# K and Q of tiles 4 to 15 projected with the tokens as the stationary operand, and laid out by transposing DMAs

## The chip, the cores and the metric

The kernel runs on one core of a Trainium2 chip. The metric is the device time of one execution in microseconds (us). The core has five engines with an instruction queue each: PE (matrix multiplication), ACT (activation functions, copies out of PSUM), DVE (element-wise vector work), POOL (a slower vector engine that can't read PSUM) and SP, which here does nothing but issue DMAs. Every queue is executed in its order: an instruction that waits holds up all those behind it on its engine.

## The reference: what is computed

One layer with two branches over x of 2048 rows (S) and 448 columns (D). Both branches are modulated by vectors that come from c: `sa, ca, ga, sb, cb, gb`, the six slices of `silu(c) @ w_mod`.

```python
h = _layernorm(x) * (1 + ca) + sa
q, k, v = h @ wqkv                      # 16 heads of 28 columns
scores = q k^T * 28 ** -0.5             # key j for row i only if 0 <= i - j < 256
o = softmax(scores) v
x = x + ga * (o @ wo)
h = _layernorm(x) * (1 + cb) + sb
z = gelu(h @ w_in)                      # 1792 columns; z1 the first 896, z2 the last
g = w_sp @ layernorm(z2) + b_sp         # w_sp: 2048 x 2048, over the rows
x = x + gb * ((z1 * g) @ w_out)
```

## The kernel before

**Tiles and stages.** The rows are cut into 16 tiles of 128; four tiles make a block (`tb`, 0 to 3). The attention window of 256 keys lets a tile see itself and the two tiles before it. There is one kernel-wide program, and its stages overlap:

1. Loads, modulation vectors, layernorm of x. For tiles 4 to 15 the normalised rows (`xn`) are brought into the layout with columns on partitions (`hT`) by a transposing DMA per tile (named h1 below; `turn`, line 465), and the modulation is applied to `hT` per block (lines 730 and 732). Tiles 0 to 3 are transposed on PE.
2. Projections. Weights for Q and K lie in `WQK`, where each head of 28 columns is padded to 32 so that a head starts on a partition that is a multiple of 32. The weights are the stationary operand and the tokens stream past: the result comes out with head columns on partitions, as the scores need it. Q of tiles 4 to 15 is made per block, four groups of four matmuls of 512 tokens (line 763, evicted into `qT` at 772 or 773), and copied once more into `QBD`, a block-diagonal arrangement for one part of the scores (lines 790 and 791). K is made per tile, 16 matmuls of 128 tokens (line 821), and evicted into `KT` (833 or 834). V has the tokens stationary and the weights streaming, four matmuls of 448 columns per tile (line 841), and is evicted into `Vaug` (845 or 846).
3. Attention of tile j, in two halves of eight heads: score matmuls (line 956, and 967 for a part that takes `QBD`; 926 for tiles 0 and 1), the exponential on ACT (line 912), a mask multiplication on DVE (973 and 993), the product with V (line 1000), division by the row sum (1014 and 1016), a transposing DMA of the result into `hT` (named o below), the product with wo (line 1026, `mo`), the residual sum (1030), the second layernorm, and another transposing DMA into `hT` (named h2).
4. The mixer. Line 1120 makes z2, line 1141 makes z1. w_sp comes from DRAM by 32 transposing DMAs of 128 x 1024, 16 into `wspA` and 16 into `wspB`. The matmuls over rows (line 1166) start when all of z2 and `wspA` are there; line 1185 is the product with w_out.

**Memory.** Most of the on-chip memory is shared by things that live at different times. `wspA` overlays `qT` and `QBD` in its first half, `wspB` overlays `KT` and `PT`.

**What sets the order.** Nothing is scheduled at run time. The kernel lists its operations (`Sched.add`; 1148 of them), with the engines that could run each, and what each depends on. `PLAN` is a text that gives the finished order: `a`, `d`, `t`, `p` and `s` stand for ACT, DVE, POOL, PE and SP, the number is the operation's place in the list, and numbers behind a dot choose buffers. `order()` hands each engine its operations in that order, `waits()` puts in the semaphore waits. So a new PLAN moves work between ACT, DVE and POOL and within every queue. SP's part of the old PLAN, from the first transpose on, in words (`h1_4`: normalised rows of tile 4 into `hT`; `o_0`: attention output of tile 0; `h2_0`: second normalisation of tile 0; `wA`, `wB`: slices of w_sp; in brackets, plain loads):

```
h1_4 h1_6 h1_7 h1_5 (x3) h1_8 h1_10 (wo) o_0 wA11 h1_9 o_1 h1_11 (winh1) wA14 o_2 wA13 o_3 (winh0) h1_13
(win1) o_4 h1_15 h1_12 h1_14 o_5 o_6 (win0) h2_0 wA15 o_8 o_7 (win2) h2_2 wA10 o_9 h2_1 o_10 h2_3 h2_6 o_11
h2_4 o_12 o_13 h2_7 o_14 h2_5 (wout) wA5 wA6 o_15 h2_8 h2_9 h2_10 h2_11 wB4 wA4 wA3 h2_12 h2_14 h2_13 wA12
h2_15 wA8 wA2 wA7 wA9 wA0 wB8 wA1 wB15 wB9 wB14 (bsp) and the eleven other wB
```

Of the kernel before, what the change touches and what calls it, by code (L numbers as in the profile page):

```python
# [12 lines left out]
a0 t30 d24 s1 d27 d26 d25 d23 d22 p51.1 t31 p60.3 s2 t32 p52.2 t35 p59.0 s4 p61.1 p55.0 s6 a3 p58.0 p63.0 a5  # L13
s10 t36 p40.1 a7 s8 p69.2 a9 p75.3 d114 s12 p65.1 p53.0 t33 d112 p68.2 s11 t34 p54.3 d115 p77.0 d113 p50.3 s13
a41 p71.0 t116 a43 p46.0 s15 d117.0 t29 p74.2 d118.3 p62.0 p64.2 p47 a42 a44 p57.0 p48.1 d106 d86 p76.0 p49
a107 t104 p129.6 p67.3 d87 d105 p126.4 t37 a130 p82.3 p56.3 t111 p84.1 d127 p81.1 p73.1 a131 p83.3 p66.0 d128
t38 p72.0 p141.1 d110 d121 p78.0 a108 t109 p70.2 p150.3 d119 p142 d122 d120 p79.2 d184 p151 t123 a143 p138.0
a152 t28 d125.2 p139 d124.3 p85.0 p147.6 d178 a140 p132.2 d185 p148 d182 a133 p144.7 d179 d180 p135.1 a134
p153.0 d183 a136 d181 p371.0 d246 t186 a137 p145 d248 p154 a372.4 t39 p165.1 d187.3 t190 d242 s194 p166 t188
a149 t192 d45 p377.0 a146 d373 p156.6 d167 a378.6 t189.1 p157 d244 p159.7 t191.2 a158 p395.0 d193.0 a155 s196  # L20
d379 p172.6 a396.5 d249 d247 p173 d243 p175.1 a174 s197 p160 d88 t89 d245 a397 p176 d168 p94.0 t250 p95 d177
s195 a171 p402.0 a161 d96 t254 p97.1 t256 a403.1 p98 d398 s14 d375 p162.7 d400 p374.0 p163 a404 d381 p90.0 d99
p376 d201 a199 p422.0 d198 d251.0 p380 p382 d200 p91 s258 a423.0.0 p211.1 d93 d92 d407 d170 d252 p212 p218.0
d255.1 t253.2 a164 d383 s260 p429.0 d169 a213 t257.3 p219 a430.3 p399.1 p205.1 s16 d220 p206 d384.2 p202.0
d306 s385 p203 a207 d426 p401 p447.0 a204 p208.1 s804 a448.4.1 d310 p209 d405 p227.0 d431 p228 s259 t102
p424.1 p406 p408 a425 p454.0 d229 a210 d409 p427.0 d312 a455.1 p230.0 t101 d410.1 p221.1 p231 d216 d214 d451
# [223 lines left out]
def bass_adaLN_cond__sliding_block__mixer_gmlp__prompt_kernel(  # L250
# [84 lines left out]


    QBD, _, qbd_bytes = alloc("QBD", [128, 2, 4, 2, 256], BF16, at=wspA_off)
    qT, _, qt_bytes = alloc("qT", [128, 2, 4, 512], BF16, at=wspA_off + qbd_bytes)
    assert qbd_bytes + qt_bytes <= NT * HS * 2

    z2, z2_off, z2_bytes = alloc("z2", [128, NT, FH], BF16)
# [927 lines left out]
```

## Time and profile before

| | |
|---|---|
| three runs | 276.32, 274.94, 275.12 us; median 275.12 |
| profiled execution, first to last instruction | 273.2 us (its own time is given as this span; 1.9 us less than the median of the runs) |
| busy: PE, ACT, DVE, POOL | 98%, 46%, 59%, 41% of the span |
| transposing DMAs into `hT` | 28 from `xn` and `xn2`, 16 from `o_sb` |
| transposing DMAs of w_sp | 32 |

How to read it: the profile is one execution, its times are microseconds from the first instruction. A line such as L821 is a line of the kernel. In the windows each engine has its busy time in a stretch, with the number of its instructions in brackets. PE's busy time counts a matmul until its last result is out, so single matmuls overlap and a mean of 0.2 us for one does not mean that it holds PE for so long; how long a group holds PE is read from the chain of waits, where each piece lasts until the next one begins. In the timeline of SP a row is the issue of a DMA, with its start, its length on SP and, where rows of one kind are merged, their number; the landing is told by tile.

### The profile page before, as it was taken

The page shows a single profiled execution, that of the slowest core. Times are in us where ns is not written, and L with a number is a line of the kernel's source. Part 1 is how long each engine was busy: PE and PEld are TensorE (multiplying, and loading weights), DVE is VectorE, ACT ScalarE, POOL GpSimd, SP SyncE. Part 2 cuts the span into 40 slices and gives each one's busy share as a digit, 9 for nine tenths or more (in the row PEclk, how much of TensorE's full clock was granted, in tenths as well). Part 3 has the DMA queues.
Part 4 walks back from the last instruction along what each step waited for, and adds up shares of the span by engine and source line. Part 5 has one row for each costly group of instructions (what it writes and reads, how often), then busy time and mean ns, then how long its engine had stood idle before and what let it go on. Part 6 is the DMA issues. An engine that isn't in the chain of part 4 may idle for free.

```text
span 273.2 us, 8371 instructions
## 1 busy us (share of the span) xinstructions
PE 267.1 (98%) x3741; PEld 155.3 (57%) x3751; DVE 160.4 (59%) x344; ACT 126.4 (46%) x149; POOL 111.4 (41%) x147
## 2 busy tenths in 40 slices
PE   8999999999999999999999999999999999999996
PEld 6976676777667866554554444444444444444453
DVE  3798999989889999949889210221222022152244
ACT  5799999899989988567666400000000000000000
POOL 6455298305033286547448003354543023061330
PEclk9999999999999999999999999999999999999999
DMA  7999846453234573957789996000000000001003
GB/s 209 299 244 132 127 103 122 122 101 109 64 103 67 91 73 72 185 117 134 117 176 175 217 186 118 0 0 0 2 0 0 0 2 0 34 17 36 34 34 118
DMA packets 67301, 25.54 MB, mean 93 GB/s; under 512 B 58497, under 2 KB 66178, under 8 KB 67266
## 3 DMA queue, kind: packets, MB, share of 16 engines
q1 hardware_dynamic: 66016, 24.02, 44.5%
q10 hardware_dynamic: 1250, 0.99, 1.3%
q8 instruction: 29, 0.48, 0.7%
q14 instruction: 6, 0.05, 0.1%
HBM read 9.01 MB, written 1.84 MB: 40 GB/s over the span
## 4 chain that ended last, share of the span: by engine, by line
PE 80%; ACT 8%; DMA 6%; DVE 3%; SPq 2%; issue 1%
PE ps L1166 35%; PE ps L1120 8%; PE ps L1141 8%; PE ps L1185 8%; ACT PW L912 6%; DMA wmodB<-in_w_mod_dram 6%; PE ps L1000 5%; PE ps L956 4%; PE ps L1026 4%; PE ps L763 3%; PE ps L821 2%; PE ps L841 2%; DVE PT L973 1%; ACT QBD L790 1%; PE ps L967 1%
## 5 line engine op out<-in xcount | busy, mean ns | idle before, releaser
L1173 POOL TENSOR_TENSOR z1T<-tmpg,z1T 128x512 bf16<-128x512 bf16 x28 | 32.0, 1152 | 77.3 <-DVE tmpg L1170 77.3
L912 ACT ACTIVATE PW<-ps 128x2048 bf16<-128x2048 f32 (+1 forms) x42 | 59.9, 1452 | 5.4 <-PE ps L956 3.9
L1170 DVE TENSOR_TENSOR tmpg<-ps,bsp_bc 128x512 bf16<-128x512 f32 x28 | 18.9, 689 | 73.8 <-PE ps L1166 62.6
L1166 PE MATMUL ps<-wspB,z 128*128 128x512 bf16 x219 | 49.7, 379 | 0.3
L1166 PE MATMUL ps<-wspA,z 128*128 128x512 bf16 x219 | 49.1, 379 | 0.4 <-issue 0.2
L633 POOL TENSOR_TENSOR rs_all<-mv_all,neghalf 128x1 f32<-128x1 f32 (+2 forms) x37 | 22.5, 635 | 45.6 <-DVE mv_all L631 45.6
L1166 PEld LDWEIGHTS ps<-wspA,z 128*128 128x128 bf16 x224 | 21.8, 98 | 26.6 <-issue 0.4
L1166 PEld LDWEIGHTS ps<-wspB,z 128*128 128x128 bf16 x224 | 21.9, 98 | 26.2
L973 DVE TENSOR_TENSOR PT<-PW,mask 128x2048 bf16<-128x2048 bf16 x28 | 34.0, 1219 | 0.0
L1000 PE MATMUL ps<-Vaug,PT 128*128 128x32 bf16 x496 | 25.8, 177 | 0.0
L1000 PEld LDWEIGHTS ps<-Vaug,PT 128*128 128x128 bf16 x496 | 22.9, 96 | 3.3 <-issue 0.4
L1120 PE MATMUL ps<-w_in,hT 64*128 64x448 bf16 x224 | 22.0, 349 | 0.0
L1185 PE MATMUL ps<-w_out_g,z1T 128*128 128x448 bf16 (+2 forms) x119 | 22.0, 341 | 0.0
L1141 PE MATMUL ps<-hT,w_in 64*128 64x512 bf16 x196 | 22.0, 376 | 0.0
L1000 PE MATMUL ps<-Vaug,PW 128*128 128x32 bf16 x224 | 21.2, 176 | 0.0
L629 DVE BATCH_NORM_STATS2 st_all<-z 128x6 f32<-128x448 bf16 x32 | 18.4, 608 | 4.4 <-ACT z L1127 4.3
L629 DVE BATCH_NORM_STATS2 st_all<-x_sb 128x6 f32<-128x448 bf16 x32 | 19.2, 614 | 2.7 <-DMA x_sb<-in_A_x_dram 2.5
L1195 DVE TENSOR_TENSOR fin<-ps,x_sb 128x448 bf16<-128x448 f32 (+1 forms) x16 | 9.5, 612 | 16.7 <-PE ps L1185 11.6
L1000 PEld LDWEIGHTS ps<-Vaug,PW 128*128 128x128 bf16 x224 | 17.9, 96 | 1.9
L821 PE MATMUL ps<-hT,WQK 112*128 112x128 bf16 x256 | 18.7, 219 | 0.0
L1149 ACT ACTIVATE z1T<-ps 128x512 bf16<-128x512 f32 x28 | 14.5, 603 | 8.8 <-PE ps L1141 8.7
L956 PE MATMUL ps<-qT,KT 32*128 32x128 bf16 (+5 forms) x1344 | 17.1, 197 | 0.9 <-ACT PW L912 0.6
(108 smaller groups left out, 355.0 us busy)
## 6 DMA issues: line engine op xcount, KB each, us to landing
wmodB<-in_w_mod_dram SPq DMA_DIRECT2D x1, 1568.0 KB, 15.3
out_dram<-fin SPq DMA_DIRECT2D x14, 112.0 KB, 1.7
x_sb<-in_A_x_dram SPq DMA_DIRECT2D x3, 448.0 KB, 7.9
w_in<-in_B_w_in_dram SPq DMA_DIRECT2D x3, 448.0 KB, 4.2
w_out_g<-in_B_w_out_dram SPq DMA_DIRECT2D x1, 784.0 KB, 6.4
bsp_bc<-in_B_b_sp_dram SPq DMA_DIRECT2D x1, 512.0 KB, 5.3
x_sb<-in_A_x_dram SPq DMA_DIRECT2D x2, 224.0 KB, 4.9
hT<-xn SPq DMA_TRANSPOSE x28, 2.9
```

The source lines that it names most:

```text
L629: st = [dve(0.62, lambda e, t=t, o=12 - 6 * (n - ci), s=s: e.bn_stats(st_all[:, slot, t, o:o + 6], s()), deps(t), prio) for ci, s in enume ...
L633: return pool(0.4 + 0.15 * len(tiles), lambda e: e.tensor_tensor(rs_all[:, slot, a:b], mv_all[:, slot, a:b, 1], neghalf[:, 0:b - a], ALU.pow),
L821: km = lambda g, kc, start, stop, h=h, t=t: lambda e: e.matmul(ps[:, h.slot[0], g * 128:(g + 1) * 128], lhsT=WQK[0:CP, kc, 16 + 4 * g:20 + ...
L912: ex = act(xdur, lambda e, out_ap=out_ap, in_ap=in_ap: e.activation(out_ap(), in_ap(), ACT.Exp, scale=SCALE), [s] + list(after), v - 8.0 + ...
L956: fm.append(lambda e, hm=hm, qi=qi, key=key, kn=kn, lo=lo, hi=hi, col=col, p0=p0, t=t, j=j: e.matmul(ps[p0:p0 + kn, hm.slot[t], col:col + ...
L973: mk2 = lock_d(1.2, lambda e, hp=hp, at_w=at_w, pad=pad, at_f=at_f, cols=cols, j=j: e.tensor_tensor(cols(hp.slot[0] * 2048, [[256, 8], [12 ...
L1000: fns.append(lambda e, hp=hp, hO=hO, hi=hi, bi=bi, kb=kb, hd=hd, nb=nb, a=at[hi][bi], p_of=p_of: e.matmul(ps[:, hO.slot[0], 32 * hd:32 * h ...
L1120: return lambda e, kc, p0, start, stop: e.matmul(ps[:, hs[t % 2].slot[hf], 0:D], lhsT=hT[p0:p0 + 64, kc, t * 128:(t + 1) * 128], rhs=w_in[ ...
L1141: return lambda e, kc, p0, start, stop: e.matmul(ps[:, hs[b // 2].slot[b % 2], :], lhsT=w_in[p0:p0 + 64, kc, ft * 128:(ft + 1) * 128], rhs ...
L1166: m = pe(16 * MMS, [lambda e, h=h, si=si, ft=ft, tb=tb: e.matmul(ps[:, h.slot[0], :], lhsT=z2[:, si, ft * 128:(ft + 1) * 128], rhs=(wspA i ...
L1173: u = pool(1.16, lambda e, ht=ht, ft=ft, tb=tb: e.tensor_tensor(z1T[tb][:, ft, :], tmpg[:, ht.slot[0], :], z1T[tb][:, ft, :], ALU.mult), [ ...
L1185: return [lambda e, ft=ft: e.matmul(ps[:, h.slot[0], 0:hi - lo], lhsT=z1T[t // 4][:, ft, (t % 4) * 128:(t % 4 + 1) * 128], rhs=w_out_g[:, ...
```

## The change

- For tiles 4 to 15, K and Q are projected like V: the 128 tokens of a tile are stationary and 448 unpadded weight columns stream past, four matmuls each. The weights are taken straight from where they were loaded (`wq_st`, which gets a place of its own).
- The results have tokens on partitions. K is evicted, with its heads spread to 32 columns, into a staging tile `kst` (two of them), and a transposing DMA of 128 x 512 lays it into `KT`. Q is evicted in two parts, of 224 columns each, into a staging tile `qst` of ten blocks of 128 columns, in which the block-diagonal arrangement is already spread out among zeros; a transposing DMA of 128 x 1280 lays it into `qring`. The QBD copies of these tiles go.
- `KT` becomes a ring of eight tiles, Q a ring of four. K of tile t waits for the scores that used its place, and so does Q.
- `qT` and `QBD` are kept for tiles 0 to 3, whose projections stay as they were; they now overlay part of `w_in`, so two loads of `w_in` wait for the scores of tiles 0 to 3.
- The first eight slices of `wspA` overlay the Q ring and wait for all scores. Five `wspA` slices had been issued before attention output 14; now it is two.
- ACT zeroes one half-size `QBD` instead of two; POOL zeroes the two `qst` and the padding of the two `kst`.
- Rules that paced the old projections (`PACE`, `LEAD`) go. PLAN is new: the first loads stay in the old order, everything later was searched anew. There are 1175 operations. SP's part, from the first transpose on (`k_4`, `q_4`: K and Q of tile 4):

```
h1_4 h1_5 h1_7 h1_6 (wo) h1_11 h1_10 q_6 q_4 h1_8 h1_9 k_4 o_0 o_1 k_5 q_5 (winh1) q_7 k_6 o_2 h1_12 o_3 k_7
q_8 h1_13 q_9 h1_14 k_8 h1_15 (winh0) q_10 k_9 (win1) q_11 o_5 o_6 o_4 k_11 k_10 wA14 h2_1 o_7 wA13 q_12 o_8
q_13 k_12 (win0) o_9 (win2) k_13 h2_3 q_14 h2_0 q_15 o_10 k_14 h2_4 h2_2 o_11 k_15 o_12 o_13 h2_5 h2_7 h2_6
o_14 wA4 (wout) h2_9 h2_8 wA11 o_15 h2_11 wA5 wA8 h2_10 wA12 wA10 h2_12 h2_14 h2_15 h2_13 wA7 wA9 wB4 wA0
wB8 wA6 wA15 wA1 wA2 wB15 wA3 wB9 wB14 (bsp) and the eleven other wB
```

The core of the diff (the PLAN is left out, and the removed per-block projection is cut):

```diff
-    KT, kt_off, kt_bytes = alloc("KT", [128, 4, S], BF16)
+    KR, QR, QB_N = 8, 4, 10
+    KT, kt_off, _ = alloc("KT", [128, 4, KR * 128], BF16)
+    wq_st, _, _ = alloc("wq_st", [128, DC, 2 * D], BF16)
+    kst = [alloc("kst0", [128, H, 32], BF16)[0]]
...
+    qring, _, qr_bytes = alloc("qring", [128, QR, QB_N, 128], BF16, at=wspA_off)
+    qst, _, qs_bytes = alloc("qst", [128, 2, QB_N * 128], BF16, at=wspA_off + qr_bytes)
...
+    t_qsz = [pool(0.8, lambda e, i=i: e.memset(qst[:, i, :].bitcast(F32), 0.0), prio=-60.0) for i in range(2)]
+    t_ksz = [pool(0.2, lambda e, i=i: e.memset(kst[i][:, :, DH:32], 0.0), prio=-60.0) for i in range(2)]
...
-            mms = [lambda e, h=h, g=g, kc=kc, tb=tb: e.matmul(
-                ps[:, h.slot[0], :], lhsT=WQK[0:CP, kc, 4 * g:4 * g + 4, :].rearrange("p a b -> p (a b)"),
-                rhs=hT[0:CP, kc, tb * 512:(tb + 1) * 512], start=(kc == 0), stop=(kc == DC - 1)) for kc in range(DC)]
...
+                def by_tokens(part, h, t=t, evs=evs, v=v):
+                    return pe2(4 * MMD, [lambda e, kc=kc: e.matmul(
+                        ps[:, h.slot[0], 0:D], lhsT=hT[0:CP, kc, t * 128:(t + 1) * 128], rhs=wq_st[0:CP, kc, part * D:(part + 1) * D],
+                        start=(kc == 0), stop=(kc == DC - 1)) for kc in range(DC)], [evs, (t_wk, t_wq)[1 - part]], v + 1, [h])
...
+                K_ready[t] = turn("d_k%d" % t, lambda t=t: KT[:, :, t % KR * 128:(t % KR + 1) * 128], lambda hs=hs: kst[hs.slot[0]][:].rearrange("p h e -> p (h e)"), [ev], v + 1)
...
+                    q_evs.append(either(
+                        0.37, lambda e, q_in=q_in, q_to=q_to: e.activation(q_to(), q_in(), ACT.Copy),
+                        0.35, lambda e, q_in=q_in, q_to=q_to: e.tensor_copy(q_to(), q_in()), [m, t_qsz], v + 1, [] if odd else [hs]))
...
+                Q_ready[t] = turn("d_q%d" % t, lambda t=t: qring[:, t % QR], lambda hs=hs: qst[:, hs.slot[0], :], [q_evs], v + 1, lat=1.6)
...
+    for t in range(8, NT):
+        K_ready[t].deps.update(x for i in range(t - KR, t - KR + 3) for x in S_of[i])
+        Q_ready[t].deps.update(S_of[t - QR])
+    for op in t_win_l[:2]:
+        op.deps.update(x for i in range(4) for x in S_of[i])
+        op.deps.update(q_dma)
```

More of the change, by code (lines that the diff above doesn't have):

```diff
@@ L18 @@
[L18 to L22, printed above, removed]
@@ L1020, in bass_adaLN_cond__sliding_block__mixer_gmlp__prompt_kernel @@
         hO.until += [rec, t_o]
[L1022 to L1023 removed]
+        oe = turn("d_oT%d" % j, lambda j=j: hT[:, :, j * 128:(j + 1) * 128], lambda ho=ho: o_sb[:, ho.slot[0], :], [t_o, hT_used[j]], v - 9.0)
         ho.until.append(oe)
```

298 lines of the change are left out of this document (136 added, 162 removed).

## The prediction

> **What bounds the kernel now.** I read the page first, then busy times by windows, the chain of waits, and the timeline of SP, which issues the transposing DMAs.
>
> ```profile
> span 273.2 us, 8371 instructions
> ...
> PE 267.1 (98%) x3741; PEld 155.3 (57%) x3751; DVE 160.4 (59%) x344; ACT 126.4 (46%) x149; POOL 111.4 (41%) x147
> ```
> ```profile
> 40.00:60.00 20.00, 19.48 (x576) 14.28 (x577) 18.06 (x35) 18.11 (x19) 8.64 (x9) 1.00 0.56 118
> 60.00:80.00 20.00, 19.75 (x589) 14.28 (x588) 17.88 (x32) 18.26 (x18) 4.27 (x6) 1.00 0.31 76
> 80.00:100.00 20.00, 19.36 (x629) 15.29 (x626) 19.74 (x40) 18.17 (x18) 9.45 (x16) 1.00 0.55 93
> ```
>
> The page's time is one execution of 273.2 us; the median of three runs is 275.12, so 1.9 us lie outside the span, and I add my difference to 275.12. The windows (length, then busy PE, weight load, DVE, ACT, POOL, clock, share of the DMA engines) show attention filled by PE, with DVE and ACT over 88% busy beside it and the DMA engines half used. PE's idle time is 0.52, 0.25 and 0.64 us in 20: what is taken from DVE or ACT alone can give back 1.4 us in these 60 at most. What is taken from PE counts in full, if everything that feeds PE keeps step.
>
> ```profile
> 26.58 1.04 PE ps L763 x4
> ...
> 53.23 0.90 PE ps L821 x16
> ...
> 65.25 0.76 PE ps L841 x4
> ...
> 68.75 0.87 PE ps L763 x4
> ...
> 101.94 0.61 PE ps L956 x32
> ...
> 152.73 10.74 PE ps L1166 x49
> ```
>
> In the chain of waits (start, length) a tile's K projection takes 0.90 us of PE (L821, 16 matmuls), a tile's quarter of a block's Q projection 0.87 (L763), and the V projection, which has its tokens stationary already, 0.76 (L841). At 101.94 stands the first score group of the last tile, tile 15; from it PE runs almost without a gap to 152.73, the first matmul with w_sp, 50.8 us later. Everything behind that is unchanged.
>
> **PE.** K and Q of tiles 4 to 15 become two projections of V's form. K falls from 0.90 to 0.76, Q from 0.87 to 0.76: 0.25 us in each of 12 tiles, 3.0 us, if PE stays the bound.
>
> **Evictions.**
>
> ```profile
> L846 DVE CAST Vaug<-ps 128x448 bf16<-128x448 f32 x6 | 3.6, 604 | 0.2 <-PE ps L841 0.2
> L834 DVE CAST KT<-ps 128x512 bf16<-128x512 f32 x5 | 3.4, 679 | 1.9 <-PE ps L821 1.7
> L791 DVE COPY QBD<-qT 32x512 bf16<-32x512 bf16 x7 | 3.3, 472 | 0.2
> ```
>
> Per tile before, at DVE's prices: one K of 512 columns (0.68), a quarter of four Q of 512 (0.68), a quarter of four QBD copies (0.47): 1.83 us. After: one K of 448 columns (0.60) and two Q halves of 224. The first two rows differ by 75 ns in 64 columns, so a half costs about 0.34: 1.28 in all. Twelve tiles save 6.6 us over DVE and ACT together. I count it at nothing, since PE's idle time allows 1.4 us; that end goes into the range.
>
> **Zeroing at the start.** ACT's second QBD fill goes, and POOL gets four memsets behind its first `rs_all`, ahead of the small `o_sb` memset and a copy into WQK.
>
> ```profile
> 1.66 1.21 POOL L499 MEMSET Vaug<- 128x768 bf16 x1
> ...
> 5.80 0.26 POOL L491 MEMSET o_sb<- 128x192 bf16 x1
> 8.41 0.56 POOL L617 COPY WQK<-wq_st 112x448 bf16<-112x448 bf16 x1 [2.36 <-DMA wq_st<-in_A_wqkv_dram]
> ```
>
> Two of 640 words and two of 64 columns cost between 4 x 0.26 and 2 x 1.21 + 2 x 0.26, 1.0 to 2.9 us, under 2.36 us in which POOL waited for a load. Their cover is that load; if it came earlier, or the memsets took the upper price, the first K matmuls would start up to 0.6 us later. I take nothing, the nearer row being the short one.
>
> **SP, the queue of the transposes.** All DMAs of this stretch are issued by SP, in one order. The change adds 24 transposes: 12 of K (four blocks of 128 x 128, like those into hT) and 12 of Q (ten blocks). Each waits for its evictions, and behind it in SP's order wait transposes of normalised rows, attention output and w_sp, and through them hT, `mo` and the last stage; the score groups wait for the new ones themselves.
>
> ```profile
> 16.65 7.39 SPq L465 DMA_TRANSPOSE hT<-xn  x4
> ...
> 30.57 1.19 SPq L465 DMA_TRANSPOSE hT<-o_sb  x1
> 31.80 1.83 SPq L465 DMA_TRANSPOSE wspA<-in_B_w_sp_dram  x1
> ...
> 65.32 0.58 SPq L432 DMA_DIRECT2D w_in<-in_B_w_in_dram  x1
> ...
> 87.59 1.20 SPq L465 DMA_TRANSPOSE hT<-o_sb  x1
> 88.87 1.88 SPq L465 DMA_TRANSPOSE hT<-xn  x1
> 91.20 1.19 SPq L465 DMA_TRANSPOSE hT<-o_sb  x1
> 92.44 2.88 SPq L465 DMA_TRANSPOSE hT<-xn  x2
> 95.36 1.27 SPq L465 DMA_TRANSPOSE hT<-o_sb  x1
> 97.05 2.15 SPq L465 DMA_TRANSPOSE hT<-xn  x1
> ...
> 104.77 1.55 SPq L465 DMA_TRANSPOSE hT<-xn  x1
> 106.36 1.27 SPq L465 DMA_TRANSPOSE hT<-o_sb  x1
> ...
> 116.48 5.19 SPq L465 DMA_TRANSPOSE hT<-xn  x4
> ...
> 143.20 1.29 SPq L465 DMA_TRANSPOSE wspA<-in_B_w_sp_dram  x1
> ...
> 149.38 16.93 SPq L465 DMA_TRANSPOSE wspB<-in_B_w_sp_dram  x11
> ```
> ```profile
> L465 SPq DMA_TRANSPOSE hT<-xn x28: 1188/1265/2212, 16.6 to 132.7; - x28
> ...
> DMA to landing us min/median/max: 2.3/3.0/6.6
> ```
>
> Four transposes in a row took 5.19 us at 116.48: with the gap behind, 1.31 us of SP for each, whatever else is free. A load takes 0.58, 0.62 with its gap. Between the first transpose at 16.65 and that of attention output 14 at 106.36 the old order has 38 transposes and seven loads, 54 us of 90: SP mostly waits. The new order has 60 and six there, 82 us, and PE means to be done with the stretch in 87.
>
> Does a Q transpose of ten blocks cost SP 1.31, or 2.5 times that? wspA's, of eight blocks, took 1.29 at 143.20, against 1.27 for four: I take 1.31 and keep the other end as a rival.
>
> Some issues are longer: 1.88 at 88.87, 2.15 at 97.05. Of the 33 transposes from 30.57 to 106.36 eight took over 1.5 us, the first at 31.80, the last at 104.77, and together 4.7 over their share: 0.14 for each of the 33. A queue that never pauses can't dodge these.
>
> The sum follows SP to the K transpose of tile 15, the last input of the score group at 101.94. Ahead of it, from 16.65, stand 54 transposes and six loads: 54 x 1.31 + 6 x 0.62 = 74.5. The first Q transpose, of tile 6, is the eighth in the order: by count 25.1. Its input can't be there: Q of this block starts at 26.58 on PE, and 0.76 of matmuls, the pipeline and an eviction half bring it to about 28.1. SP stands for 3.0. The longer issues add 54 x 0.14 = 7.6. So it is issued at 16.65 + 74.5 + 3.0 + 7.6 = 101.7 and lands 3.0 later by the median, 104.7: 2.8 us behind the old 101.94, while PE, 3.0 ahead, stands idle for some 5 us over tiles 12 to 15. Its queue is in order, so all work behind the score group waits too. Counted by the chain's spacings, the new order keeps 0.6 us less PE work behind this point. That gives 2.8 - 0.6 = 2.2 us over before, 277.3.
>
> At 116.48 transposes are spaced by their issue and not by their movement, and that is the ground of this sum. The Trainium skill (DMA: Bandwidth & Descriptors, Issuing engines are not separate DMA queues) says that the sequencer's time to initiate a DMA is usually small beside the DMA; here it is 1.27 of a landing of 3.0. By that rule SP would not be a bound, and the first rival would hold.
>
> For movement: eleven wspB transposes of 256 KB took 16.93 us, 1.54 each, so eight blocks move in at most that and ten in 1.9. A tile's K and Q then add 0.8 + 1.9 = 2.7 us of all DMA engines, 32 us in 85, upon shares of 0.31 to 0.56. That stays under one, but landings get later than the median; the range takes that in. The Trainium skill (Advanced Engine Details and Errata, X-Bar Transpose (TRN2)) expects 350 to 400 GB/s; the row gives 170. By its figure the addition would be half as long, and landings would hold to the median.
>
> Loads of w_in now wait for the scores of tiles 0 to 3; those are over before the first is due, and their place in SP's order is in the count.
>
> **Rivals.** *SP keeps step, PE stays the bound.* If pauses before SP's early inputs are shorter, the long issues are rarer, or the K transposes are ready with spare time, PE gets its 3.0 us: 272.1; with the 1.4 us of idle time, 270.7. For it: 82 us of SP fit into 87. Against: that leaves 5 for 3.0 of waiting and 60 x 0.14 = 8.4 of long issues. It decides at an issue of tile 15's K by about 96. Chance 0.31.
>
> *Saving and lag cancel.* The forecast with a lag of SP that is 1 to 3 us smaller, 274.3 to 276.3, no change. Chance 0.25.
>
> *The transposes of w_sp arrive last.*
>
> ```profile
> L465 SPq DMA_TRANSPOSE wspA<-in_B_w_sp_dram x16: 1166/1301/4177, 31.8 to 143.2; - x16
> ...
> DMA to landing us min/median/max: 3.0/3.9/6.7
> ```
>
> Behind attention output 14 the old order has 24 issues to the last wspA transpose, in 143.20 - 106.36 = 36.8 us; landing by 147.1, it had 5.6 us to spare before 152.73. The new one has 27 (early wspA transposes have moved behind): 41.4. With SP late, output 14 goes at 16.65 + 82.3 + 3.0 + 8.4 = 110.4, the last wspA at 151.8, landing at 155.7 to 158.5; PE would want it at 152.7 + 2.2 = 154.9. That is 0.8 to 3.6 us beyond the forecast, 278.1 to 280.9. It decides from a landing later than PE's 154.9. Chance 0.12, beside the forecast's own 0.29.
>
> *A ten-block issue costs 2.5 times a four-block one:* 12 x 1.9 = 23 us, 298. The 1.29 speaks against it; 0.03.
>
> That the change does not save PE time I exclude: V's form is in the trace.
>
> **How the numbers follow.** A difference under 0.5% (1.4 us) can't be told from none here. The edges are 273.7 and 276.5, and the forecast, 277.3, stands over the upper one: slower 0.29 + 0.12 + 0.03 = 0.44, same 0.25, faster 0.31. Slower is likelier than same, since the two terms that carry the lag, landing and long issues, can grow with a fuller queue and hardly shrink. The range runs from 271.8, short of the first rival's best end, to 280.3, inside the third's; some 0.2 is left out at both ends. The forecast's own range, over a lag of SP that is up to 2 us shorter or longer, is 275.3 to 279.3.
>
> **What would show it.** Right: SP's timeline without pauses from 45 to 105; transposes into KT landing 3 us or more after issue; among PE's waits, the score groups for DMA into KT or the Q ring, several us in all; K and Q projections at 0.76 us a tile; tile 15's first scores between 103 and 106; the first w_sp matmul at 153 to 156. Wrong: SP waiting for several us in each 20, PE at 19.5 or more in each window to 100, and the first w_sp matmul before 151. If PE waits for wspA ahead of its first w_sp matmul, it is the third rival.

## The result, and the profile after

The changed kernel is slower: 299.5 us median against 275.7 for the kernel before, beside it on the same chip. Medians are over all runs, while ratios leave out disturbed, slower runs: two of the four here (301.5 and 301.8), two of four in e16_vector_later and one each in e6_k_alone, e7_sixteen_less and e17_start_mended. The ratio is 1.073 (95% interval 1.065 to 1.081), 20 us. The profiled execution of the changed kernel took 294.6 us, and its page begins:

```profile
span 292.8 us, 8134 instructions
...
PE 271.6 (93%) x3597; PEld 149.6 (51%) x3607; DVE 159.9 (55%) x340; ACT 121.1 (41%) x144; POOL 119.4 (41%) x159
```

PE's share fell from 98% to 93%. The windows show where, in the columns of the prediction's (length, then busy PE, weight load, DVE, ACT, POOL, granted clock, share of the DMA engines):

```profile
40.00:60.00 20.00, 16.73 (x511) 10.99 (x498) 16.96 (x34) 15.38 (x16) 11.04 (x11) 1.00 0.70 114
60.00:80.00 20.00, 17.05 (x504) 11.73 (x499) 17.14 (x27) 16.35 (x14) 8.57 (x8) 1.00 0.99 151
80.00:100.00 20.00, 17.79 (x424) 10.84 (x424) 15.69 (x31) 12.23 (x12) 2.90 (x6) 0.91 0.82 133
```

From 40 to 100 us PE now stands for 3.3 + 2.9 + 2.2 = 8.4 us, where it stood for 1.4. Its waits (us in all, times, longest), the largest and those that the prediction named:

```profile
PE ps L1010 <- DVE KT L796: 4.0, 1, 4.0
PE ps L966 <- DMA KT<-kst: 3.0, 2, 1.8
...
PE ps L1165 <- DMA wspA<-in_B_w_sp_dram: 1.4, 1, 1.4
```

The first is new and stands at the start; the second is a score group that waits for the transposed K; the third is the first matmul with w_sp (L1165) waiting for a slice of w_sp. SP's timeline (start, length on SP, merged issues), at the start and at the end of the attention part:

```profile
16.61 6.65 SPq L471 DMA_TRANSPOSE hT<-xn  x4
23.30 0.58 SPq L399 DMA_DIRECT2D wo_g<-in_A_wo_dram  x1
29.55 2.50 SPq L471 DMA_TRANSPOSE hT<-xn  x2
33.80 3.96 SPq L471 DMA_TRANSPOSE qring<-qst  x2
...
109.71 1.67 SPq L471 DMA_TRANSPOSE KT<-kst  x1
111.42 2.58 SPq L471 DMA_TRANSPOSE hT<-xn  x2
114.04 1.85 SPq L471 DMA_TRANSPOSE hT<-o_sb  x1
115.93 1.28 SPq L471 DMA_TRANSPOSE KT<-kst  x1
```

The first Q transpose goes out at 33.80 and the last K transpose at 115.93. Between them an issue begins some 0.04 us after the one before has ended; all that goes beyond this is 0.4 us together. At the start SP still pauses, 5.7 us ahead of 29.55.

What the trace shows best is when each score group starts on PE. From the timelines of PE, in us (the experiments in the columns are told below):

| first matmul of | before | after | e4 | e5 | e15 | e9 | e17 | e11 |
|---|---|---|---|---|---|---|---|---|
| tile 2 | 25.1 | 34.1 | 33.1 | 24.7 | 35.6 | 26.9 | 26.0 | 26.5 |
| tile 4 | 37.1 | 45.3 | 45.2 | 36.7 | 47.5 | 45.0 | 39.9 | 45.5 |
| tile 9, second half | 69.8 | 83.3 | 78.0 | 78.2 | 88.8 | 81.7 | 79.2 | 77.8 |
| tile 15 | 101.9 | 119.3 | 110.1 | 114.6 | 125.6 | 120.5 | 116.2 | 108.7 |
| w_sp | 152.7 | 172.4 | 160.9 | 169.5 | 180.2 | 173.1 | 171.7 | 162.4 |
| span | 273.2 | 292.8 | 281.4 | 290.2 | 300.9 | 293.8 | 292.4 | 283.1 |

The changed kernel loses 8.2 us by tile 4, 9.2 more by tile 15, 2.3 more by the first matmul with w_sp, and nothing behind it. So there are two losses to explain, an early one and a long one, and my theory had only the second.

The early one can be read in the chain of waits (start, length) of the changed kernel:

```profile
8.29 14.77 DMA x_sb<-in_A_x_dram
...
23.09 0.63 DVE st_all L637
...
26.80 0.58 DVE KT L796
27.37 0.05 issue
27.42 0.29 PE ps L1010 x4
```

DVE's new order has the statistics (L637) of tiles 13 to 15 ahead of masks and of the eviction of K of tile 2 (L796). These tiles belong to the last third of x, whose load lands at 23.1, so DVE stands for 5.5 us in front of it with ready work behind, and PE behind DVE for 4.0. So my theory, A below, has two parts: an early loss by the order at the start, and a long one by SP's full queue. The main rivals: the loss is PE's own, in the new projections and evictions; the issues are long because of Q's ten blocks; or SP's pauses would take the new issues in, and the order alone is at fault. All ratios are to the kernel before, run beside it on the same chip, with a 95% interval; "us more" is worked out from them.

### The profile page after: what moved, and what is told of

It reads as the page before. It is cut to its first block, busy times and chain, and to the rows that moved or that the text cites. A ratio compares the mean times of both kernels' runs of the same rounds, so it can differ in the third digit from the quotient of the medians.

```text
span 292.8 us, 8134 instructions
## 1 busy us (share of the span) xinstructions
PE 271.6 (93%) x3597; PEld 149.6 (51%) x3607; DVE 159.9 (55%) x340; ACT 121.1 (41%) x144; POOL 119.4 (41%) x159
## 4 chain that ended last, share of the span: by engine, by line
PE 48%; DMA 18%; DVE 11%; POOL 8%; SPq 8%; issue 3%; ACT 2%; POOLq 0%; DVEq 0%
PE ps L1165 33%; PE ps L1184 7%; SPq L471 6%; DMA x_sb<-in_A_x_dram 5%; DMA hT<-o_sb 3%; DMA KT<-kst 3%; DMA hT<-xn 3%; DVE PT L983 2%; POOL xn L659 2%; DVE st_all L637 2%; POOL hT L1060 2%; PE ps L805 2%; ACT PW L922 2%; POOL rs_all L641 2%; DMA wspA<-in_B_w_sp_dram 2%
## 5 line engine op out<-in xcount | busy, mean ns | idle before, releaser
L1165 PE MATMUL ps<-wspA,z 128*128 128x512 bf16 x219 | 49.1, 379 | 1.6 <-DMA wspA<-in_B_w_sp_dram 1.4
L1165 PE MATMUL ps<-wspB,z 128*128 128x512 bf16 x219 | 49.7, 379 | 0.3
L641 POOL TENSOR_TENSOR rs_all<-mv_all,neghalf 128x1 f32<-128x1 f32 (+2 forms) x37 | 24.9, 697 | 46.8 <-DVE mv_all L639 44.5
L1165 PEld LDWEIGHTS ps<-wspA,z 128*128 128x128 bf16 x224 | 21.8, 98 | 27.8 <-issue 1.6
L1165 PEld LDWEIGHTS ps<-wspB,z 128*128 128x128 bf16 x224 | 21.9, 98 | 26.2
L983 DVE TENSOR_TENSOR PT<-PW,mask 128x2048 bf16<-128x2048 bf16 x28 | 34.8, 1255 | 0.8 <-ACT PW L922 0.8
L1010 PEld LDWEIGHTS ps<-Vaug,PT 128*128 128x128 bf16 x496 | 22.7, 96 | 9.1 <-DVE KT L796 4.4
L805 PE MATMUL ps<-wq_st,hT 112*128 112x448 bf16 x96 | 24.9, 382 | 0.6 <-DVE kst L818 0.6
L637 DVE BATCH_NORM_STATS2 st_all<-x_sb 128x6 f32<-128x448 bf16 x32 | 18.9, 613 | 8.1 <-DMA x_sb<-in_A_x_dram 8.0
L637 DVE BATCH_NORM_STATS2 st_all<-z 128x6 f32<-128x448 bf16 x32 | 18.2, 605 | 4.0 <-ACT z L1126 4.0
L966 PE MATMUL ps<-qring,KT 32*128 32x128 bf16 (+5 forms) x1152 | 15.4, 201 | 5.2 <-DMA KT<-kst 3.0
L966 PEld LDWEIGHTS ps<-qring,KT 32*32 32x32 bf16 (+1 forms) x1152 | 12.1, 92 | 13.2 <-ACT PW L922 5.4
L1035 PE MATMUL ps<-wo_g,hT 112*128 112x448 bf16 x64 | 17.1, 378 | 1.6 <-DMA hT<-o_sb 0.7
```

The costliest lines, as they stand in the source:

```text
L637: st = [dve(0.62, lambda e, t=t, o=12 - 6 * (n - ci), s=s: e.bn_stats(st_all[:, slot, t, o:o + 6], s()), deps(t), prio) for ci, s in enume ...
L641: return pool(0.4 + 0.15 * len(tiles), lambda e: e.tensor_tensor(rs_all[:, slot, a:b], mv_all[:, slot, a:b, 1], neghalf[:, 0:b - a], ALU.pow),
L805: return pe2(4 * MMD, [lambda e, kc=kc: e.matmul(ps[:, h.slot[0], 0:D], lhsT=hT[0:CP, kc, t * 128:(t + 1) * 128], rhs=wq_st[0:CP, kc, part ...
L966: fm.append(lambda e, hm=hm, qi=qi, key=key, kn=kn, lo=lo, hi=hi, col=col, p0=p0, t=t, j=j: e.matmul(ps[p0:p0 + kn, hm.slot[t], col:col + ...
L983: mk2 = lock_d(1.2, lambda e, hp=hp, at_w=at_w, pad=pad, at_f=at_f, cols=cols, j=j: e.tensor_tensor(cols(hp.slot[0] * 2048, [[256, 8], [12 ...
L1010: fns.append(lambda e, hp=hp, hO=hO, hi=hi, bi=bi, kb=kb, hd=hd, nb=nb, a=at[hi][bi], p_of=p_of: e.matmul(ps[:, hO.slot[0], 32 * hd:32 * h ...
```

## The experiments

### The early order in the old kernel: e4_old_with_fault and e4b_x_load_alone

```diff
 the kernel before, PLAN
-SP:  ... (x2) (wmodB) h1_4 h1_6 h1_7 h1_5 (x3) ...
+SP:  ... (x2) (wmodB) (x3) h1_4 h1_6 h1_7 h1_5 ...
-DVE: ... screp mask ... bn0_12 mask_2.0 bn0_14 ...
+DVE: ... screp bn0_15 bn0_13 bn0_14 mask ...        (e4_old_with_fault only)
```

> The kernel before with the order of the changed kernel at the start alone: the last third of x is loaded ahead of the first transposes on SP, and VectorE's statistics of tiles 13, 14 and 15 stand early, ahead of masks and of the evictions of tiles 2 and 3. Nothing of the change itself is in it. Theory A (this order alone delays the start by 6 to 9 us): 281 to 284 us. Rival B (the delay at the start is a consequence of the new projections, or is made good later): within 2 us of the kernel before.

Measured: 283.6 us, ratio 1.026 (1.021 to 1.032), 7.2 us more: theory A. DVE's timeline has the wait in it, and PE's waits show what it costs:

```profile
23.79 1.68 DVE L627 BATCH_NORM_STATS2 st_all<-x_sb 128x6 f32<-128x448 bf16 x3 [5.55 <-DMA x_sb<-in_A_x_dram]
```
```profile
PE ps L839 <- DVE qT L801: 5.4, 1, 5.4
```

By the traces its score groups are 8.1 us late at tile 4 and still 8.1 at w_sp: PE, which is the bound of the old kernel, never makes good what it lost once.

> The kernel before with the last third of x loaded ahead of the first four transposes, and nothing else moved (e4_old_with_fault without the early statistics). Theory A (the load takes the DMA engines ahead of the transposes of tiles 4 to 7, which then land 2 us later, and VectorE's place in line adds the rest): 1 to 3 us more than the kernel before, where the early statistics with it made 7.5. Rival B (the load's place alone makes the loss): 6 us more or worse.

Measured: 277.0 us, 1.0045 (1.001 to 1.008), 1.2 us more. So the place of the load is nearly free; the three DVE instructions that wait for it are the fault.

### SP's load in the old kernel: e5_old_with_24 and e5b_old_with_12

```diff
 the kernel before
+    spares = [pool(0.2, lambda e: e.memset(spare[:, 0, :], 0.0), prio=-60.0)]
+    for i in range(24):
+        spares.append(turn("d_spare%d" % (i % 4), lambda i=i: spare[:, 1 + i % 4, :].rearrange("p (b k) -> p b k", k=128), lambda: spare[:, 0, :], [spares[0]] + spares[-4:][:1], 0.0))
 PLAN, SP: one ahead of each of o_0 to o_11, one behind the next issue after it (e5b: 12, the first kind only)
```

> The kernel before with 24 more transposes on SP, two for each of tiles 4 to 15, of 128 x 256 in a spare piece of memory that nobody reads; each of the four destinations is written again only after the transpose before it on that place. PE, ACT and DVE have the old work in the old order. Theory A (the number of issues on SP sets the end of the attention part: 24 times 1.31 us, or 31 us, come on top of the 60.5 us that 46 issues took in 91 us): SP has no pause left from 30 to about 105 us, score groups start to wait for transposes, and the time is 3 to 10 us more than the kernel before. Rival B (SP's pauses take the 24 issues in, and what the changed kernel loses is lost in its own order and waits): within 2 us of the kernel before.

Measured: 291.7 us, 1.056 (1.052 to 1.060), 15.5 us more, beyond the range that I expected. Nobody reads what these transposes write, and PE, ACT and DVE do the old work in the old order. PE's waits, then the 24 issues by tile (ns on SP min/median/max, first and last start), then SP's timeline in the same stretch that the old kernel had with pauses:

```profile
PE ps L1026 <- DMA hT<-o_sb: 7.8, 4, 2.7
PE ps L1000 <- DVE o_sb L1016: 2.6, 1, 2.6
```
```profile
L465 SPq DMA_TRANSPOSE spare<-spare x24: 1167/1245/2178, 29.5 to 115.5; - x24
```
```profile
45.98 1.24 SPq L465 DMA_TRANSPOSE spare<-spare  x1
47.26 1.27 SPq L465 DMA_TRANSPOSE hT<-o_sb  x1
48.57 2.60 SPq L465 DMA_TRANSPOSE wspA<-in_B_w_sp_dram  x1
51.22 2.54 SPq L465 DMA_TRANSPOSE spare<-spare  x2
53.80 1.88 SPq L465 DMA_TRANSPOSE hT<-o_sb  x1
```

The attention outputs of tiles 2 and 3 (rows 47.26 and 53.80) were issued at 42.2 and 47.1 in the kernel before. They now go out when the queue lets them, not when they are ready, and PE waits for such outputs in four places. Two blocks cost SP as much (1.25 us) as four (1.27): it is the number of issues that counts. This is the clearest result of the study: 24 small transposes that nobody needs, without anything else of the change, cost three quarters of its loss.

Not all of the 15.5 us is waiting. The granted clock (the column behind POOL in the windows) falls behind such waits, to 0.76 in the mean from 60 to 80 us:

```profile
60.00:80.00 20.00, 16.98 (x449) 12.29 (x448) 12.91 (x24) 13.61 (x14) 2.96 (x5) 0.76 0.69 92
```

Over the span it is 0.971; 0.029 x 290.2 = 8.4 us is an estimate, at most, of what PE lost by it.

The prediction quoted the Trainium skill (DMA: Bandwidth & Descriptors, Issuing engines are not separate DMA queues), that the time to initiate a DMA is usually small beside the DMA. For these transposes the trace disagrees: an issue takes 1.25 to 1.27 us of SP, and a landing 3.0 by the median.

> The kernel before with 12 more transposes on SP, one ahead of each of the first twelve transposes of attention outputs, half of e5_old_with_24, which cost 15.6 us. Theory A (SP has pauses of some 30 us between 16 and 107 us, 46 issues taking 60.5; 12 more take 15.7 us and fit, so that the price comes only past a threshold): 0 to 4 us more than the kernel before. Rival B (each issue costs in proportion, wherever it stands, since it delays the transpose behind it): 7 to 9 us more.

Measured: 278.7 us, 1.011 (1.005 to 1.017), 3.0 us more. Half the issues cost a fifth of the price. Two things go together here: of some 15 us that twelve issues take on SP 3.0 come through to the time, and the granted clock stays at 1.000, where 24 brought it down to 0.971. Where between 12 and 24 the price rises, two points can't tell.

### Both at once: e15_old_both

The edits of e4_old_with_fault and e5_old_with_24 in one kernel.

> The kernel before with both of its loads from the experiments at once: the start of e4_old_with_fault (the last third of x first, the statistics of tiles 13 to 15 early; 7.5 us) and the 24 more transposes of e5_old_with_24 (15.6 us). PE's work is the old one. Theory A (the changed kernel's time is made of these two, which overlap: while SP's queue is what paces the score groups, a late start is partly hidden by it): 292 to 297 us, about the changed kernel's. Rival B (they are independent and add up): 298 to 300 us.

Measured: 301.6 us, 1.090 (1.086 to 1.095), 24.9 us more, against 7.2 + 15.5 = 22.7 for the two alone. This is rival B, even above its 298 to 300 us: in the old kernel they add up, and the overlap of theory A falls. Two faults that have nothing to do with the projections make more than the changed kernel's whole loss of 20 us; part of the difference may be what its projections save, which this run doesn't show.

### The early order in the changed kernel: e1_start, e9_start2, e17_start_mended

```diff
 the changed kernel, PLAN
 e1_start            DVE: bn0_15, bn0_13, bn0_14 and an aggregation behind bn0_12
 e9_start2           DVE: all four bn0 behind mask_2.0, masks of tiles 0 and 1 ahead of the modulation of block 1
                     SP:  (x3) behind h1_6;  PE: Q_6, Q_4, K_4 behind PV of tile 0
 e17_start_mended    as e9_start2, and DVE: the bn0 of 12 to 15 behind the masks of tile 3; two of wo_g to POOL
```

> The changed kernel with four VectorE instructions moved: the statistics of tiles 13, 14 and 15 stand behind those of tile 12, and no longer ahead of the masks and of the K and V evictions of tiles 2 and 3. Nothing else differs. Theory A (a fault at the start: VectorE waits 5.5 us for the last third of x at 23 us, the first Q transpose is issued at 33.8 us instead of the 28.1 us that I had worked out, and SP, full from there on, carries that to the end): 6 to 9 us less than the changed kernel, so about 286 to 289 us. Rival B (only the load of SP counts; its queue would have been just as late with an earlier start, since the K and Q evictions feed it at PE's pace): within 2 us of the changed kernel.

Measured: 295.5 us, 1.070 (1.064 to 1.076): no gain, rival B's number. The second group of tile 1 came 4.5 us earlier, but PE then waited 3.1 us for the modulated tiles 4 to 7, whose projections stand ahead of tile 2 in its order.

> The order of the first 35 us put back to what the kernel before does there, in the changed kernel: the last third of x is loaded behind the first four transposes again, the statistics of tiles 12 to 15 stand behind the first mask of tile 2, the masks of tiles 0 and 1 ahead of the modulation of tiles 4 to 7, and the projections of Q_6, Q_4 and K_4 behind the score group of tile 2 on PE. Moving the statistics alone (e1_start) brought the second group of tile 1 from 29.1 to 24.6 us, but the first group of tile 2 only from 34.1 to 32.2, since PE then waited 3.1 us for the modulated tiles 4 to 7. Theory A (the start is lost by this order, and SP's queue is the second loss): the first group of tile 2 at 25 to 27 us, but SP, full from its first Q transpose on, gives only part of it back at the end: 288 to 292 us. Rival B (the start is lost by the new projections whatever the order): the first group of tile 2 stays behind 30 us and the time within 2 us of e1_start's 295.5.

Measured: 295.8 us, 1.074 (1.069 to 1.080). Tile 2 starts at 26.9, as theory A said, but the time is rival B's, and tile 4 starts at 45.0, as late as ever. The loss had moved on. Neither run had mended the start, so neither tells whether a mended start helps. The chain of waits of e11_start2_less, which has the same start, shows where it went:

```profile
36.66 2.13 DVE st_all L638 x4
...
39.23 0.62 DVE o_sb L1027
...
40.02 0.24 DVE qst L837
...
40.61 0.61 DVE wo_g L610
...
42.06 1.30 DVE wo_g L610
43.35 0.54 DVE kst L819
43.89 1.00 DVE PT L984
```

From 35 to 45 us the chain lies on DVE nearly without a break: statistics and weight products (L610) stand among the evictions of Q and K that PE waits for.

> The kernel of e11_start2_less (no K and Q transposes of tiles 8 to 15, the start put back; the scores of these tiles read what tiles 0 to 7 left in the rings) with VectorE relieved between 34 and 46 us: the statistics of tiles 12 to 15 (2.2 us and four aggregations) stand behind the masks of tile 3, and the two weight products that took 2.0 us there are on GpSimd. In e11_start2_less the chain of waits from 34 to 45 us lies on VectorE nearly without a break, and PE waited 1.5 us for a Q eviction there. Theory A (what was left, 7.5 us over the kernel before, is mostly VectorE's queue at this place): 2 to 5 us less than e11_start2_less, 278 to 281 us. Rival B (it is spread over many small waits of an order made for other times): no more than 1.5 us less.

Measured, without most of the transposes: 281.6 us median; the ratio, from two runs of 279.0 and 279.7 us, is 1.011 (1.006 to 1.016) where e11_start2_less had 1.026 (1.021 to 1.030), about 4 us less. Theory A: DVE's queue was the second early fault.

> The changed kernel complete, with all 24 K and Q transposes, and with both places of its early order mended as in e16_vector_later: the start put back, VectorE's statistics of tiles 12 to 15 and two weight products taken out of 30 to 46 us. Neither e1_start nor e9_start2 had mended the early loss: their first score group of tile 4 starts at 44.5 and 45.0 us, the changed kernel's at 45.3, the old one's at 37.1. Theory A (the two losses add, as in e15_old_both): 3 to 5 us less than e9_start2, 290.5 to 293 us. Rival B (here SP's queue, not PE, decides from about 35 us on, and takes the gain back): no more than 1.5 us less than e9_start2's 295.8.

Measured: 296.0 us, 1.071 (1.060 to 1.081): rival B's number, no gain. But it is only in part rival B's mechanism. The first Q transpose now goes out at 30.15, 3.7 us earlier than in the changed kernel; tile 4's scores start 5.3 us earlier, and tile 15's still 3.1. So the stretch that SP fills takes back 2.2 us, and the rest is lost behind tile 15: the first matmul with w_sp is only 0.6 us earlier. Rows of PE's waits in e17_start_mended (the first stands ahead of tile 15, the other two behind it), and of its w_sp transposes by tile:

```profile
PE ps L968 <- DMA KT<-kst: 5.3, 3, 2.0
PE ps L1121 <- POOL hT L1062: 2.2, 1, 2.2
...
PE ps L1037 <- issue: 1.4, 1, 1.4
```
```profile
L473 SPq DMA_TRANSPOSE wspA<-in_B_w_sp_dram x16: 1298/1301/2556, 78.7 to 166.3; - x16
...
DMA to landing us min/median/max: 3.2/4.1/5.3
```

Behind tile 15 PE stands 1.4 us ahead of a product with wo (`issue`: the profile shows nothing that it waited for), runs at a granted clock of 0.50 from 121.5 to 124.9 us, and waits 2.2 us for POOL (L1062, the modulation of the second normalisation). It waits for no slice of w_sp. But the last slice is issued at 166.3 and lands at 171.6, just ahead of that matmul at 171.7, so SP's queue is a second limit close behind: without those waits PE would have met it almost at once. This is read from the trace; no run took these limits away one by one.

### Less of the new load: e3_four_blocks, e7_sixteen_less, e11_start2_less, e13_none

```diff
 e3_four_blocks     e1_start with
-    Q_ready[t] = turn(..., qring[:, t % QR], ... qst[:, hs.slot[0], :], ...)
+    Q_ready[t] = turn(..., qring[:, t % QR, 0:4], ... qst[:, hs.slot[0], 0:512], ...)
 e7_sixteen_less    e1_start, e11_start2_less  e9_start2, with
+    K_ready[t] = ev if t >= 8 else turn(...);  Q_ready[t] = q_evs[1] if t >= 8 else turn(...)
 e13_none           e9_start2 with the same for t >= 4
```

> The kernel of e1_start with the Q transposes cut from ten blocks of 128 columns to four; the other six blocks of the Q ring are zeroed once, so the scores that read them are made from zeros (this part of Q's layout is left out; the number of PE's instructions and of SP's issues is the same). Theory A (a ten-block transpose makes the issue behind it take 2 to 3 us instead of 1.31, which is most of the 16 us by which the 52 issues between the first Q transpose and the last K transpose exceed 66.0 us): 8 to 14 us less than e1_start, and hardly an issue over 2 us behind a Q transpose. Rival B (the issues are long because of their number or of other traffic): within 3 us of e1_start.

Measured: 294.0 us, 1.062 (1.054 to 1.069), 1.5 us less than e1_start by the medians: rival B. The issues over 1.75 us are as many (13) as in e1_start, and SP's way from the first Q transpose to the last K transpose takes 82.3 us (83.4 there). My idea that a ten-block transpose makes the next issue long falls; six tenths of Q's bytes less change next to nothing. Full DMA engines are not what holds SP either: from 60 to 80 us their share is 0.73 here, 0.96 in e1_start, and the queue takes as long.

> The kernel of e1_start without the K and Q transposes of tiles 8 to 15 (sixteen of the 24; projections and evictions stay, the scores of these tiles read what tiles 0 to 7 left in the rings, so this part of the layout is left out). PE's instructions are the same, SP has 44 transposes before the last score groups where it had 60. Theory A (SP's queue sets the end of the attention part, and the projections by tokens do save PE the 3.0 us that I had worked out): 270 to 275 us, at or a little under the kernel before. Rival B (the loss is in PE's own new work or in the evictions, for instance a lower granted clock or later evictions): 282 us or more, and no more than 5 us under e1_start.

Measured: 285.5 us, 1.031 (1.024 to 1.038), by the ratios 11 us less than e1_start. Neither theory's number: the sixteen transposes are worth 11 us, and 8.4 are left for something else. (With the transposes go their landings and the waits for staging tiles and ring places; that issues alone can cost this much is shown by e5_old_with_24.) The chain of waits shows two projections by tokens at full clock:

```profile
86.12 1.52 PE ps L806 x8
```

That is 0.76 us for four matmuls, what the prediction took from V's.

> The kernel of e9_start2 without the K and Q transposes of tiles 8 to 15, as in e7_sixteen_less (the scores of these tiles read what tiles 0 to 7 left in the rings; this part of the layout is left out). Theory A (two losses and one gain: the start, SP's queue, and 2.6 us of PE saved in the K and Q projections, which held PE 21.9 us before and 19.3 us in e7_sixteen_less): with both losses gone the time comes to the kernel before's or under it, 273 to 278 us. Rival B (there is a third loss on PE, in evictions or in the clock): 281 us or more.

Measured: 283.2 us, 1.026 (1.021 to 1.030), 13 us less than e9_start2 and 7 more than the kernel before: rival B, a third loss. About 4 of the 7 us are DVE's queue of above (e16_vector_later).

> The kernel of e9_start2 without any transpose of K or Q: projections and evictions of all tiles stay, the rings of tiles 4 to 15 are zeroed once, and the scores read zeros there (the layout of K and Q of these tiles is left out). e11_start2_less, with 8 of the 24 left, stood 7.5 us above the kernel before. Theory A (what is left there is SP's load of tiles 4 to 7, whose eight transposes stand in the busiest stretch of the queue, 28 to 60 us): 273 to 277 us, the PE time saved then shows. Rival B (what is left is the order of the plan, made for other times: evictions, masks and modulations that PE waits for): no more than 3 us under e11_start2_less, 280 us or more.

Measured: 283.3 us, 1.026 (1.022 to 1.031): rival B. No transpose of tiles 4 to 7 is needed to keep the early loss. (Zeroing the rings cost this kernel some 2 us at its start: its first score group stands at 19.8 us, in e11_start2_less at 17.4.) With no new transposes its score groups are 9.7 us behind the old kernel's at tile 4 and 6.9 at the first half of tile 14: 2.8 regained, which fits the saving of 3.0. At w_sp they are 9.6 behind again, so behind tile 14 the new order loses as much without any K or Q transpose.

### K alone in the old order: e6_k_alone and e6b_k_placed

```diff
 the kernel before; K of tiles 4 to 11 and 13 to 15 by tokens, as in the change (KT a ring of eight, wq_st beside it, two kst)
 SP, e6_k_alone:   each T k_t right behind its eviction's place in PLAN: ... o_7 k_13 (win2) k_14 h2_2 wA10 k_15 o_9 ...
 SP, e6b_k_placed: by the times of the trace before:                 ... o_7 (win2) h2_2 wA10 k_13 o_9 k_14 h2_1 o_10 h2_3 k_15 ...
```

> The kernel before, in its own order, with K alone projected with tokens stationary, for tiles 4 to 11 and 13 to 15: eleven transposes of K on SP, each right behind its eviction, K in the ring of eight tiles, the unpadded weights in a place of their own; Q as before. The K projections of tiles 5 and 6, and of 13 and 14, have changed places in the order, so that each eviction ends over 5.5 us ahead of its score group. Theory A (the projections by tokens do save PE time, 16 x 56 ns less 4 x 189 ns = 0.14 us for a tile, as long as no wait is added; the loss came from the order and from SP's full queue): PE is not made to wait, and the time is 1 to 2 us less than the kernel before. Rival B (moved K transposes cost more than they save even with SP half empty, by later landings or by a lower clock after each new wait): 1 us more than the kernel before, or worse.

Measured: 284.6 us, 1.028 (1.024 to 1.033), 7.7 us more: rival B. SP's timeline has the reason:

```profile
75.65 1.30 SPq L466 DMA_TRANSPOSE wspA<-in_B_w_sp_dram  x1
81.31 2.51 SPq L466 DMA_TRANSPOSE hT<-o_sb  x2
89.42 1.19 SPq L466 DMA_TRANSPOSE KT<-kst  x1
...
99.11 2.03 SPq L466 DMA_TRANSPOSE hT<-o_sb  x1
```

SP stands from 83.8 to 89.4 for one K transpose whose eviction is not done, and the attention output behind it, and behind two more K transposes, goes out at 99.1 instead of 87.6.

> The kernel of e6_k_alone with the eleven K transposes moved on SP to where the kernel before has its pauses, by the times of its trace and behind the end of each eviction there. In e6_k_alone SP stood 4.4 and 5.6 us at 77 to 89 us for an attention output and for the K transpose of tile 13, which waited for its eviction, and the next attention output went out at 99.1 us instead of 87.6. Theory A (most of the 8 us came from a transpose that waits in the queue ahead of ready ones): 275 to 279 us. Rival B (the number of issues alone did it): 282 us or more.

Measured: 279.1 us, 1.011 (1.006 to 1.016): 3 us more, theory A. Most of the 7.7 us came from where the transposes stood in the queue (all eleven were moved, so no single one is shown to be at fault). The granted clock went with it, 0.982 in e6_k_alone and 0.999 here; 0.018 x 285.0 = 5.1 us is an estimate, at most, of that part. What is left is what e5b_old_with_12 cost with twelve issues. K by tokens saves 0.14 us of PE for a tile and brings an issue of 1.3 us, and in the better of the two orders that still didn't pay. No version that I tried is faster than the kernel before.

## Why the prediction was wrong, step by step

The direction that I held likeliest, slower, was right, and SP's queue is the mechanism of the larger part. The early loss and the loss of clock were not in the prediction at all, and the size was wrong by a factor of nine, 20 us for 2.2. In the sum's own terms: it put tile 15's scores at 104.7, and they start at 119.3, 14.6 us later, of which 5.7 are the first Q transpose and 8.5 the longer issues; it put the first matmul with w_sp at 154.9, and it starts at 172.4, a further 2.9.

- **PE saves 3.0 us: right in the chain, never seen in the time.** A projection takes 0.76 us for four matmuls (e7_sixteen_less), and the 2.8 us regained in e13_none fit. But this holds only at full clock: see the last section.
- **A wait on PE costs its length: a term put at nothing without a reason.** The sum let PE stand idle for some 5 us and then go on at full clock. The changed kernel's granted clock is 0.977 over 292.8 us, up to 6.7 us by the estimate of the last section. How much of this lies on the path to the end is open.
- **Evictions count for nothing: right in sum, wrong in place.** DVE and ACT together were busy for 5.8 us less, near my 6.6. Where its new order puts other work among evictions, masks and statistics, PE waited: 4 us (e16_vector_later).
- **Zeroing counts for nothing: not settled.** The first score group starts at 16.9 us instead of 15.1, but profiles of variants of the old kernel have it anywhere from 14.8 to 16.8.
- **The first Q transpose at 28.1: this step failed first.** I took its time from the old kernel's PE, as if the start stayed. It went out at 33.80, 5.7 us later. The diff shows DVE's statistics of tiles 13 to 15 ahead of the masks; I had followed SP's order and not DVE's. By itself this order costs 7.2 us in the old kernel (e4_old_with_fault). With all that I mended of it in the changed kernel the transpose still goes out at 30.15 (e17_start_mended).
- **The longer issues, 0.14 us for each transpose: too small by more than half.** From the first Q transpose to the last K transpose SP took 82.1 us for 48 transposes and five loads, whose floor is 48 x 1.31 + 5 x 0.62 = 66.0: 16.1 over, 0.34 for each transpose. My term for it was 7.6. Of the 16.1, 12.2 lie in twelve issues over 1.75 us.
- **The rest of the sum held.** 101.7 + 5.7 + 8.5 = 115.9 is the issue of the last K transpose; it landed at 118.3, and tile 15's scores start at 119.3. Of the signs that I had named, the queue without pauses, the waits for K and the K transposes' late landings (3.1 us by the median) are there, and the two times are 13 to 19 us later than named.
- **Behind tile 15 nothing more: wrong by 2.3 us.** PE waits 1.4 us for a slice of w_sp, the third rival, to which I had given 0.12. It came on top of the forecast's own loss, not in its place. Nor is it the whole of this step: in e11_start2_less, with SP relieved, tile 15 to w_sp still takes 53.6 us against 50.8 before, and there PE waits 2.0 us for POOL.
- **A ten-block issue costs 2.5 times: excluded.** By tile, the Q transposes of the changed kernel:

```profile
L471 SPq DMA_TRANSPOSE qring<-qst x12: 1337/1552/2995, 33.8 to 105.3; - x12
...
DMA to landing us min/median/max: 4.5/5.1/6.8
```

The shortest, 1.34 us, is near the 1.31 that I took. Their landing, 5.1 us, is longer than the 3.0 that I took for K. Among PE's waits none for `qring` shows, so this hurt little.

- **SP keeps step (0.31): refuted** by the changed kernel's SP, which has no pause from 33.8 to 115.9 us, and by e5_old_with_24, in which 24 issues cost 15.5 us. I had counted 82 us of issues in 87 and called it a fit; a queue in order that is 94% full, each entry waiting for its input and being waited for, isn't one.

What stays open: what the last 3 us of e16_vector_later are; which of the limits behind tile 15 takes a mended start's gain; and how the loss divides between waiting and the clock that falls behind a wait.

## What to carry to other kernels

Count the issues of the engine that issues the DMAs as you count PE's time, with its own floor (here some 1.3 us for a transpose, of two blocks or ten), and take a queue in order as full well before 100%: here twelve more issues cost 3 us and 24 cost 15.5. A step that saves 0.14 us on the bound for an issue of 1.3 us did not pay here, even with its issues put into the pauses. A wait on the bound can cost more than its length, so look at the granted clock behind it. When an order has been searched anew, read the new order of every engine from its start: for each wait, ask what stands behind it that is already ready, since in the old kernel three misplaced instructions cost as much as a third of the whole loss.

## What the runs showed of the hardware

**Long issues fall on instruction fetches.** In the changed kernel all twelve transposes that took SP over 1.75 us between 33.8 and 115.9 us overlap a fetch of 16 KB on the instruction queue; there are 16 such fetches in that time, about 1 us each. In the old kernel, from 16.6 to 107 us, it is seven of seven, with 20 fetches, of which ten met issues that were not longer and three met none; in e3_four_blocks and e17_start_mended it is 13 of 13, in e1_start 12 of 13. The stretch around one such issue, 35.1 to 37.9 us of the changed kernel, by DMA queue (packets, MB, share of 16 engines):

```profile
q1 hardware_dynamic: 1156, 0.30, 117.3%
q8 instruction: 1, 0.02, 2.5%
```

The Trainium skill (Runtime: NRT & Kernel Launch, Instruction fetch mechanics) says that crossing such a 16 KB boundary is mostly hidden. If the fetches are the cause, the trace disagrees for SP's queue: the twelve issues stand 12.2 us over the floor. But this is a coincidence in time, with one exception in e1_start and ten fetches without effect in the old kernel; no run took the fetches away. In the stretch shown the transposes' own queue is busy to the full too, which could be another cause of a single long issue.

**PE is slow after it has stood, even for 2 us.** The windows of the changed kernel behind the 4.0 us wait at 27.4, with the granted clock in the column behind POOL:

```profile
28.00:34.00 6.00, 6.00 (x36) 2.35 (x34) 4.15 (x11) 2.41 (x3) 4.07 (x7) 0.52 0.20 44
34.00:40.00 6.00, 6.00 (x201) 4.55 (x204) 5.62 (x17) 5.16 (x6) 0.00 (x0) 1.00 0.93 134
```
```profile
31.46 2.70 PE ps L805 x8
```

Two projections took 2.70 us where they take 1.52 at full clock. The granted clock is 0.50 from 26.9 to 33.7 us, and again from 81.5 to 84.9 and from 102.0 to 105.4, behind waits of 2.0 and 1.8 us. Over the span the clock is 0.977, and 1.000 in the kernel before: an estimate from these two is 0.023 x 292.8 = 6.7 us at most. So a wait on PE can cost more than its length.

The Trainium skill (TensorE: Matmul & The Clock Gate, Part 1: The HAM clock gate) has half the clock after an idle window of some 3.4 us, and the full clock after as long a busy one. The trace agrees on the half, but the window need not be idle throughout: in the 3.4 us ahead of 81.5 and of 102.0 PE was busy for 1.4 and 1.6 us.
